# Weight rows loaded and split at other places of the program, and a third of one subtraction moved from GpSimd to VectorE, in a pre-LN block with dilated local attention and a squared-ReLU MLP

## The chip, the cores and the metric

The kernel runs on one core of a Trainium2 chip. The metric is device time in microseconds (us) of one execution; the median of three runs counts. Before the change it is 510.53 us (510.51 to 511.3). TensorE is called PE here, VectorE DVE, ScalarE ACT, GpSimd POOL, and SyncE, which issues nearly every DMA, SP, as in the profile.

## The reference

```
x = A_x                                              # 1 x 2048 x 512, f32
h = x + attn(layernorm(x), wqkv, wo)                 # 32 heads of 16
    # query s attends to keys s, s-2, ..., s-14; logits scaled by 16 ** -0.5,
    # those before the start are masked, softmax over the 8
h2 = h + mlp(layernorm(h), w1, b1, w2, b2)           # 512 -> 1792 -> 512
    # mlp: r = max(x @ w1 + b1, 0); (r * r) @ w2 + b2
```

## The kernel before

**Arithmetic.** Each matrix product is made of three PE products on numbers cut in two: `hi` copies a tile to the format fp32r on ACT (the high part, names ending in `_h`), `lo` subtracts that copy from the tile (the low part, `_l`), and PE adds high x high, low x high and high x low. "Splitting" a row of weights means a DMA of it to a buffer `raw`, one `hi` on ACT and one `lo` on POOL.

**Stages.** Tokens come in 16 tiles of 128.
1. The opening, 16 slots: layernorm, transposes and the q, k, v products of tiles 0 to 3, two head groups at a time.
2. Six passes of `first_phase` (`t0` = 4, 6, ... 14): the q, k, v products of two tiles each, in 12 slots numbered `m`.
3. The MLP of token blocks `u` = 0, 1, 2 (four tiles each): a slot `p` has the first product of weight column f = p (`mlp1`), the second product of f = p - 3 (`mlp2`), and at some p the attention's output product of a tile of the next block (`wo_product`).
4. The last block, `u` = 3, in another form of products.

Attention runs beside all this up to the middle of block 2: 64 units, each three DVE instructions of some 1.2 us (L339, L350, L373) and three additions on POOL (L407). q, k and v go to a DRAM buffer (`qkv_d`, from the tile `y2`, which has two buffers) and come back as windows `k`, `v`, `q`.

**What sets the order.** The order of every engine is written out by the program. A chore is put down for a slot: `at` (run at the start of the slot's end, list `due`), `midway`, `after` (run last, list `late`). `end_slot` runs `due`, then `pump`, which hands out attention until the planned DVE time reaches the planned PE time, then `late`. A chore on DVE that calls `dve(t)` therefore pushes attention back by t in the program. All DMAs but three stand in SP's one queue in the order of the program, and one whose source is not yet written holds up those behind it. Small tiles (rows of x, h, raw weights, parts) take turns in 15 buffers with the tag `row`.

**Lines of the change.** `weight_job` (L570) loads and splits one row of `wo` (4 jobs, 128x512) or of `w1` (16 jobs, 128x448); `first_phase` calls it at L1020. `split_w2` (L1069) splits row p of `w2` in slot p of block 0: `hi` to `big_h`, `lo` to a place in `big_l`, from where `stash` (L1078) stores it to DRAM one slot later for the later blocks. The place is taken again four rows later.

Of the kernel before, what the change touches and what calls it, by code (L numbers as in the profile page):

```python
# [52 lines left out]
HOLD = 1.0  # L53
XS = 6
WARM = 18


@with_exitstack
def block_kernel(ctx, tc, x, wqkv, wo, w1, b1, w2, b2, out):
    nc = tc.nc  # L60
# [39 lines left out]
    w2_h, w2_l = {}, {}  # L100

    def row(name, shape=(P, D), dt=F32):
        return work.tile(list(shape), dt, name=name, tag="row", bufs=ROWS)
# [9 lines left out]
    def at(delta, fn, *a):  # L113
        due.setdefault(now["slot"] + delta, []).append((fn, a))

    def after(delta, fn, *a):
        late.setdefault(now["slot"] + delta, []).append((fn, a))
# [4 lines left out]
    def end_slot(pe):  # L122
        now["pe"] += pe
        run(due)
        pump()
        run(amid)
        run(late)
        now["slot"] += 1
# [7 lines left out]
    def dve(t):  # L136
        now["dve"] += t
# [13 lines left out]
    def hi(dst, src):  # L151
        nc.scalar.copy(dst, src)  # L152
# [298 lines left out]
    def x_center(t):  # L451

        st = small.tile([P, 6], F32, name="st")
        mv = means[t] = small.tile([P, 2], F32, name="mv0", bufs=R)
        rs = rstd[t] = small.tile([P, 2], F32, name="rs0", bufs=R)
        nc.vector.bn_stats(st, xt[t])
        nc.vector.bn_aggr(mv, st)
        nc.vector.tensor_scalar(out=xt[t], in0=xt[t], scalar1=mv[:, 0:1], scalar2=None,
                                op0=ALU.subtract)
        dve(1.4)  # L460

    def x_rstd(t):
        mv, rs = means[t], rstd[t]
        nc.gpsimd.tensor_scalar(out=rs[:, 1:2], in0=mv[:, 1:2], scalar1=EPS, scalar2=None,
                                op0=ALU.add)
        nc.gpsimd.tensor_tensor(out=rs[:, 0:1], in0=rs[:, 1:2], in1=mhalf, op=ALU.pow)

    def x_T(t):
        tr = transposes(xt.pop(t))
        xT[t] = row("xh", (P, KB, P), F32R), row("xl", (P, KB, P), F32R)  # L470
        at(0, hi_T, tr, [xT[t][0]])
        after(0, lo_T, tr, [xT[t][0]], [xT[t][1]])
# [57 lines left out]
    def qkv_of(t, c, mid):  # L530

        ps = turn["mm"].tile("mm")
        xh, xl = xT[t]
        cs = slice(c * D, (c + 1) * D)
        mm3(ps, lambda k: xh[:, k, :], lambda k: xl[:, k, :],
            lambda k: wq_h[:, k, cs], lambda k: wq_l[:, k, cs], mid, 3 * KB // 2,
            lows_last=True)
        at(1, evac, t, 0, c, ps)

    def qkv(t, gp, mid=None):  # L540

        ps = turn["mm"].tile("mm")
        xh, xl = xT[t]
        mm3(ps[:, :3 * GP], lambda k: xh[:, k, :], lambda k: xl[:, k, :],
            lambda k: pair(wq_h, k, gp), lambda k: pair(wq_l, k, gp), mid, lows_last=t > 0)
        at(1, evac, t, gp, None, ps)
# [3 lines left out]
    def load_wqkv(gp, ks=range(KB), eng=nc.sync):  # L550
        for k in ks:
            if k % 2 == 0:
                tag = "pr" if (gp, k) in ((1, 2), (2, 0), (2, 2)) else "o"
                raws[gp] = att.tile([P, 2, D], F32, name="wraw", tag=tag, bufs=3)
            r = raws[gp, k] = raws[gp][:, k % 2, :3 * GP].rearrange("p (c n) -> p c n", c=3)
            src = wqkv[k * P:(k + 1) * P].rearrange("p (c n) -> p c n", c=3)
            eng.dma_start(r, src[:, :, gp * GP:(gp + 1) * GP])
# [9 lines left out]
    jobs = [(wo_h, wo_l, wo, k, 0, D) for k in range(KB)]  # L567
    jobs += [(w1_h, w1_l, w1, k, c * 448, 448) for k in range(KB) for c in range(4)]

    def weight_job():  # L570
        h, l, src, k, c0, cn = jobs.pop(0)
        raw = row("raw")
        nc.sync.dma_start(raw[:, :cn], src[k * P:(k + 1) * P, c0:c0 + cn])

        def split():
            hi(h[:, k, c0:c0 + cn], raw[:, :cn])
            after(0, lo, nc.gpsimd, l[:, k, c0:c0 + cn], raw[:, :cn], h[:, k, c0:c0 + cn])
        at(5, split)


    hs, hn = {}, {}
# [10 lines left out]
    def o_T(t):  # L592
        s, j = divmod(t, RI)
        pump(until=s)
        tr = transposes(o_t[s][:, j, :])
        if t % R == RI:

            ohl = att.tile([P, 2, KB, P], F32R, name="ohl", tag="o", bufs=3)
            oT[t] = ohl[:, 0], ohl[:, 1]
        else:  # L600
            oT[t] = row("oh", (P, KB, P), F32R), row("ol", (P, KB, P), F32R)
        at(0, hi_T, tr, [oT[t][0]])
        at(0, lo_T, tr, [oT[t][0]], [oT[t][1]])
# [79 lines left out]
    def wo_product(t, slots):  # L683
        ps = turn["mm"].tile("wo")
        oh, ol = oT.pop(t)
        mm3(ps, lambda k: oh[:, k, :], lambda k: ol[:, k, :],
            lambda k: wo_h[:, k, :], lambda k: wo_l[:, k, :], lows_last=t in OV)
        for n, (fn, a) in zip(slots, ((h_add, (t, ps)), (h_norm, (t,)), (add_b2, (t,)),
                                      (spill, (t,)))):
            (after if fn in (h_norm, spill) else at)(n + (fn is add_b2), fn, *a)  # L690
# [254 lines left out]
    warm = turn["tr"].tile("tr").rearrange("p (k c) -> p k c", k=KB)  # L945
    for n in range(WARM):
        nc.tensor.transpose(warm[:, n % KB, :], ident, ident)

    def start_T(t):
        x_T(t)  # L950
        run(due)
        run(late)

    def consts():
        nc.sync.dma_start(b1_sb, b1.rearrange("(f p) -> p f", p=P))
        nc.sync.dma_start(b2_sb, bass.AP(tensor=b2.tensor, offset=b2.offset, ap=[[0, P], [1, D]]))
# [20 lines left out]
    for n in range(16):  # L977
        gp, t = divmod(n, 4)
        qkv(t, gp, (lambda: start_T(t + 1)) if n < 3 else None)
        if n == 0:  # L980
            x_rstd(2)
            x_center(3)
        if n == 1:
            x_rstd(3)
        if n < 6:
            for k in (0, 1):
                at(0, hi_wqkv, n // 2 + 1, n % 2 * 2 + k)
                after(0, lo_wqkv, n // 2 + 1, n % 2 * 2 + k,
                      nc.gpsimd if k or n < 2 else nc.vector)
        if n == 1:  # L990
            load_wqkv(3)
        if n == 13:
            consts()
        if n in (5, 6, 12, 14):
            at(0, load_x, n - 1 if n < 7 else n // 2)
        if n in (8, 9):
            at(0, x_stats, n - 4)
        if n in (11, 12):
            at(0, x_norm, n - 7)
        if n in (13, 14):  # L1000
            x_T(n - 9)
        end_slot(2.09)
# [4 lines left out]
    def first_phase(t0):  # L1007
        def chores(m):
            if t0 + 3 < 16:
                if m in (0, 2):  # L1010
                    at(0, x_stats, t0 + 2 + m // 2)

                early = t0 == 12
                if m + early in ((4, 6) if t0 == R else (6, 7)):
                    at(0, x_norm, t0 + 2 + (m + early) // 7 if t0 > R else t0 + m // 2)
                if m in XT[early]:
                    x_T(t0 + 2 + XT[early].index(m))
            if t0 + 5 < 16 and m in (6, 9):
                at(0, load_x, t0 + 2 + m // 3)
            if jobs and m % 3 == 0:  # L1020
                at(0, weight_job)
            k = t0 // 2 * 12 - 72 + m
            if k == 19:
                dve(HOLD)
            for t in range(R):
                if k == OT[t]:
                    at(0, load_h, t)
                    o_T(t)
                if t in HV and k == HK[t][0]:
                    at(0, h_split, t)  # L1030
                    after(0, turn_dma, ("h", t))
                if t in HV and k == HK[t][1]:
                    at(0, turn_join, ("h", t))
                if k == WO[t]:
                    wo_product(t, (1, 3, 4, 6))
                    now["pe"] += 2.73
                if k == HT[t]:
                    (at(0, h_parts, t) if t in HV else h_T(t))
            if k in W2:
                at(0, load_w2, W2.index(k))  # L1040

        def half(m):
            end_slot(1.37)
            chores(m)

        for n in range(6):
            chores(2 * n)
            qkv_of(t0 + n % 2, n // 2, lambda: half(2 * n + 1))
            end_slot(1.37)
# [19 lines left out]
    def split_w2(f):  # L1069
        raw = raws.pop(f)  # L1070
        hi(w2_h[f], raw)
        if f < 12:
            place[f] = free.pop(0)
            w2_l[f] = big_l[:, place[f]]
            at(1, stash, f)
        after(0, lo, nc.gpsimd, w2_l[f], raw, w2_h[f])

    def stash(f):  # L1078
        nc.sync.dma_start(w2l_d[f], w2_l[f].bitcast(F32))
# [7 lines left out]
    for u in range(R - 1):  # L1087
# [45 lines left out]
        for p in range(FB + LAG):  # L1133
# [17 lines left out]
            if q >= 0:  # L1151
                f = fs[q]
# [93 lines left out]
```

## Time and profile before

| | us |
|---|---|
| median of the runs | 510.53 |
| the profiled execution | 510.24 |
| its span (first to last instruction) | 508.5 |
| PE busy | 498.6 (98%) |
| DVE busy | 375.2 (74%) |
| POOL busy | 361.4 (71%) |
| ACT busy | 305.3 (60%) |
| DMA queue of SP, share of 16 DMA engines | 68% |
| granted PE clock | 1.00 throughout |

PE counts as busy while one of several overlapping matmuls is in flight, so small stalls show less as idle time than as fewer matmuls in a stretch. The times of rows below are counted from the start of the span. A row of the timeline reads: start, duration of the group, engine, line, operation, output<-inputs, shape, count, and in brackets the idle time of that engine ahead of it with what ended it.

The stages lie at these places: the opening to 40 us, the six passes to 161 us, block 0 from 161 to 255 us, block 1 to about 340 us, block 2 to about 427 us.

### The profile page before, as it was taken

What the parts mean: (1) busy time and instruction counts of PE and PEld (TensorE: products, weight loads), DVE (VectorE), ACT (ScalarE), POOL (GpSimd) and SP (SyncE); (2) the same over time, 40 slices, a digit from 0 to 9 for tenths busy, and PEclk for the clock granted to TensorE, in tenths of its full rate; (3) what the DMA queues carried; (4) which work ended last, traced back from release to release, by engine and by line L of the source; (5) the groups of instructions that cost most, each with busy time, mean ns of one, the idle gap of its engine ahead of it and who ended that gap; (6) DMA issues with size and microseconds to landing.
All of it is one profiled execution on the core that took longest, in us unless ns stands there. A gap on an engine that the chain in (4) does not pass through costs nothing.

```text
span 508.5 us, 7542 instructions
## 1 busy us (share of the span) xinstructions
PE 498.6 (98%) x2422; PEld 420.5 (83%) x2422; DVE 375.2 (74%) x507; ACT 305.3 (60%) x558; POOL 361.4 (71%) x439
## 2 busy tenths in 40 slices
PE   8999999999999999999899999999999999999997
PEld 7998778888888887787688888888888888998986
DVE  6479899999999778986898989988951137732233
ACT  4635687577447747478454548756457847566541
POOL 5714789895776999989959777977896364685610
PEclk9999999999999999999999999999999999999999
DMA  8678889899698799789576756997572272444212
GB/s 271 189 212 204 245 290 302 245 307 303 201 228 253 253 273 278 215 216 291 166 248 207 216 147 165 257 252 244 161 173 63 80 212 83 169 123 144 64 43 83
DMA packets 109359, 102.61 MB, mean 202 GB/s; under 512 B 29448, under 2 KB 77832, under 8 KB 109320
## 3 DMA queue, kind: packets, MB, share of 16 engines
q1 hardware_dynamic: 108376, 101.61, 68.0%
q10 hardware_dynamic: 944, 0.52, 0.3%
q8 instruction: 19, 0.31, 0.2%
q14 instruction: 20, 0.16, 0.1%
HBM read 72.65 MB, written 24.25 MB: 191 GB/s over the span
## 4 chain that ended last, share of the span: by engine, by line
PE 66%; POOL 14%; DVE 2%; issue 2%; DMA 2%; ACT 1%; SPq 0%; POOLq 0%; ACTq 0%; DVEq 0%
PE mm L228 30%; PE acc L895 22%; PE wo L228 6%; PE mm L818 6%; POOL pr L407 5%; POOL rl L155 3%; POOL big_l L155 3%; PE tr L201 2%; POOL h L674 1%; DVE pr L350 1%; DMA q<-qkv_d 1%; DMA k<-qkv_d 1%; POOL o L407 1%; POOL w_x L155 1%; POOL rs L171 0%
## 5 line engine op out<-in xcount | busy, mean ns | idle before, releaser
L407 POOL TENSOR_TENSOR pr<-pr 128x512 f32<-128x512 f32 (+1 forms) x128 | 132.3, 1034 | 38.2 <-DVE pr L350 32.7
L228 PE MATMUL mm<-big_l,w_h 128*128 128x512 f32 x336 | 88.9, 391 | 0.7 <-ACT r L871 0.7
L350 DVE TENSOR_TENSOR pr<-ex,v 128x1024 f32<-128x1024 f32 x64 | 78.1, 1221 | 13.5 <-POOL o L407 10.1
L339 DVE TENSOR_TENSOR pr<-qp,k 128x1024 f32<-128x1024 f32 x64 | 76.8, 1200 | 9.3 <-ACT qp L268 8.4
L373 DVE TENSOR_REDUCE ex<-pr 128x64 f32<-128x1024 f32 x64 | 78.5, 1227 | 2.0
L228 PEld LDWEIGHTS mm<-big_l,w_h 128*128 128x128 f32 x336 | 62.8, 188 | 15.0 <-ACT r L871 2.0
L155 POOL TENSOR_TENSOR rl<-r,rh 128x512 fp32r<-128x512 f32 x42 | 55.6, 1326 | 14.9 <-ACT rh L152 14.9
L228 PE MATMUL mm<-big_l,xh 128*128 128x512 f32 (+1 forms) x208 | 55.8, 378 | 0.0
L228 PE MATMUL mm<-big_h,xh 128*128 128x512 f32 (+1 forms) x208 | 53.8, 379 | 1.3 <-ACT xh L152 1.3
L228 PE MATMUL mm<-big_h,xl 128*128 128x512 f32 (+1 forms) x208 | 52.7, 375 | 0.1
L895 PE MATMUL acc<-big_l,rh 128*128 128x512 f32 x190 | 52.2, 390 | 0.0
L895 PE MATMUL acc<-big_h,rh 128*128 128x512 f32 x190 | 52.1, 391 | 0.0
L895 PE MATMUL acc<-big_h,rl 128*128 128x512 f32 x190 | 51.7, 389 | 0.0
L871 ACT ACTIVATE r<-mm,b_sb 128x512 f32<-128x512 f32 x42 | 28.8, 685 | 33.6 <-PE mm L228 30.3
L228 PE MATMUL mm<-big_l,w_l 128*128 128x512 f32 x168 | 44.9, 389 | 0.0
L228 PEld LDWEIGHTS mm<-big_h,xh 128*128 128x128 f32 x208 | 37.6, 188 | 8.6 <-ACT xh L152 3.0
L228 PEld LDWEIGHTS mm<-big_h,xl 128*128 128x128 f32 x208 | 38.2, 188 | 6.4 <-DVE xl L155 0.5
L895 PEld LDWEIGHTS acc<-big_h,rl 128*128 128x128 f32 x190 | 35.7, 188 | 7.4
L895 PEld LDWEIGHTS acc<-big_l,rh 128*128 128x128 f32 x190 | 35.5, 188 | 7.4
L228 PEld LDWEIGHTS mm<-big_l,xh 128*128 128x128 f32 x208 | 37.5, 188 | 4.9
L895 PEld LDWEIGHTS acc<-big_h,rh 128*128 128x128 f32 x190 | 34.9, 188 | 6.7
L228 PEld LDWEIGHTS mm<-big_l,w_l 128*128 128x128 f32 x168 | 31.5, 188 | 6.6
(165 smaller groups left out, 917.8 us busy)
## 6 DMA issues: line engine op xcount, KB each, us to landing
k<-qkv_d SPq DMA_DIRECT2D x48, 288.0 KB, 3.1
v<-qkv_d SPq DMA_DIRECT2D x48, 288.0 KB, 3.6
qkv_d<-y SPq DMA_DIRECT2D x18, 512.0 KB, 5.1
big_l<-w2l_d SPq DMA_DIRECT2D x24, 256.0 KB, 3.1
xt<-in_A_x_dram SPq DMA_DIRECT2D x16, 256.0 KB, 4.7
q<-qkv_d SPq DMA_DIRECT2D x32, 128.0 KB, 3.7
h<-in_A_x_dram SPq DMA_DIRECT2D x16, 256.0 KB, 3.3
h_d<-h SPq DMA_DIRECT2D x16, 256.0 KB, 3.8
```

Source lines behind the costliest of these rows:

```text
L155: eng.tensor_tensor(out=dst, in0=src, in1=h, op=ALU.subtract)
L201: nc.tensor.transpose(tr[:, k, :], src[:, k * P:(k + 1) * P], ident)
L228: nc.tensor.matmul(ps, l(k), r(k), start=(n == 0), stop=(n == 3 * KB - 1))
L339: nc.vector.tensor_tensor(out=pr.rearrange("p i w h d -> p i w (h d)"), in0=qps["now"][:, j % 2].unsqueeze(2).to_broadcast([P, RI, W, GC]) ...
L350: nc.vector.tensor_tensor(out=p2, in1=vwin, op=ALU.mult, in0=e1[:, :, :, j * GH:(j + 1) * GH].unsqueeze(4).to_broadcast([P, RI, W, GH, DH]))
L373: nc.vector.tensor_reduce(out=lf[:, :, :, j * GH:(j + 1) * GH], in_=pr, axis=X, op=ALU.add)
L407: nc.gpsimd.tensor_tensor(out=dst, in0=p2[:, :, :w], in1=p2[:, :, w:2 * w], op=ALU.add)
L674: nc.gpsimd.tensor_tensor(out=h, in0=h, in1=b2_sb, op=ALU.add)
L818: nc.tensor.matmul(ps, sta[y][:, k], mov[x][:, k], start=(first and q == 0), stop=(last and q == len(terms) - 1), skip_group_check=True)
L871: nc.scalar.activation(r, ps, AF.Relu, bias=b1_sb[:, f:f + 1])
L895: nc.tensor.matmul(acc[j], l[:, j * P:(j + 1) * P], w[f], start=(first and n < len(js)), stop=(last and n >= len(terms) - len(js)))
```

## The change

Three edits.
- Three of the twenty weight jobs (rows 0 to 2 of `wo`) are put into the opening, at slots 4, 6 and 8, to be split four slots later. A pass has three jobs (m = 0, 4, 8) instead of four (m = 0, 3, 6, 9); the last two fall into the pass t0 = 14, which had none.
- The split of a job is run in `late`, behind the slot's attention, instead of in `due`, ahead of it.
- In block 0 the `lo` of rows f = 1, 4, 7, 10, 13 of `w2` goes to DVE instead of POOL, and 0.8 us of planned DVE time is booked for each.

```diff
+JOBS = 4, 6, 8
+JM = 0, 4, 8
...
-    def weight_job():
+    def weight_job(delay=5):
         h, l, src, k, c0, cn = jobs.pop(0)
...
-        at(5, split)
+        after(delay, split)
...
+        if n in JOBS:
+            at(0, weight_job, 4)
...
-            if jobs and m % 3 == 0:
+            if jobs and m in (JM if t0 < 14 else (0, 3, 5)):
                 at(0, weight_job)
...
-        after(0, lo, nc.gpsimd, w2_l[f], raw, w2_h[f])
+        eng = nc.vector if f % 3 == 1 else nc.gpsimd
+        after(0, lo, eng, w2_l[f], raw, w2_h[f])
+        if eng is nc.vector:
+            dve(0.8)
```

Line numbers of the changed kernel are higher by 2 in the helpers.

SP's queue in the opening, before. `qkv_d<-y` stores q, k and v of a pair of tiles, `qkv_d<-qkv_d` copies the rows ahead of the first token, `xt` is a tile of x, `k`, `q`, `v` are windows of attention.

```order
L487 DMA qkv_d<-qkv_d 2x8x64 x2
L497 DMA qkv_d<-y_90 128x3x128 x2
L247 DMA k<-qkv_d 128x704
L260 DMA q<-qkv_d 128x2x128
L247 DMA k<-qkv_d 128x704
L247 DMA v<-qkv_d 128x704 x2
L438 DMA xt<-in_A_x_dram 128x512 x2
L497 DMA qkv_d<-y_90 128x3x128 x2
L260 DMA q<-qkv_d 128x2x128
L487 DMA qkv_d<-qkv_d 2x8x64 x2
L497 DMA qkv_d<-y_90 128x3x128 x4
```

The same stretch of SP's queue with the change, from the store behind the first copy on:

```order
L575 DMA raw<-in_A_wo_dram 128x512
L499 DMA qkv_d<-y_90 128x3x128 x2
L249 DMA k<-qkv_d 128x704
L262 DMA q<-qkv_d 128x2x128
L249 DMA k<-qkv_d 128x704
L249 DMA v<-qkv_d 128x704 x2
L440 DMA xt<-in_A_x_dram 128x512 x2
L575 DMA raw<-in_A_wo_dram 128x512
L499 DMA qkv_d<-y_90 128x3x128 x2
L262 DMA q<-qkv_d 128x2x128
L489 DMA qkv_d<-qkv_d 2x8x64 x2
L575 DMA raw<-in_A_wo_dram 128x512
```

Each of the three loads stands right ahead of a store of `y`.

POOL at the start of block 0, before. `big_l<-raw,big_h` is the `lo` of a row of `w2` (the raw buffer's number tells the rows apart: 1871 is f = 0, 1980 f = 1, 2007 f = 2), `rl<-r,rh` the `lo` of a hidden column, `pr` and `o` the additions of an attention unit.

```order
L155 TENSOR_TENSOR big_l<-raw_1871,big_h 128x512
L155 TENSOR_TENSOR rl<-r,rh 128x512
L407 TENSOR_TENSOR pr<-pr 128x2x256
L407 TENSOR_TENSOR pr<-pr 128x2x128
L407 TENSOR_TENSOR o<-pr 128x2x64
L155 TENSOR_TENSOR big_l<-raw_1980,big_h 128x512
L155 TENSOR_TENSOR rl<-r,rh 128x512
```

POOL at the same place with the change (1869 is f = 0, 2007 f = 2):

```order
L157 TENSOR_TENSOR big_l<-raw_1869,big_h 128x512
L157 TENSOR_TENSOR rl<-r,rh 128x512 x2
L409 TENSOR_TENSOR pr<-pr 128x2x256
L409 TENSOR_TENSOR pr<-pr 128x2x128
L409 TENSOR_TENSOR o<-pr 128x2x64
L157 TENSOR_TENSOR big_l<-raw_2007,big_h 128x512
```

The subtraction of f = 1 has left POOL, and the next attention unit's additions stand behind the second hidden column's.

DVE in the middle of block 0, around the first `wo_product`, before. `ol` is the low part of the attention output of tile 4, `h<-wo,h` adds that product to the residual.

```order
L350 TENSOR_TENSOR pr<-ex,v 128x1024
L373 TENSOR_REDUCE ex<-pr 128x16x4
L339 TENSOR_TENSOR pr<-qp,k 128x1024
L350 TENSOR_TENSOR pr<-ex,v 128x1024
L373 TENSOR_REDUCE ex<-pr 128x16x4
L155 TENSOR_TENSOR ol<-pl,oh 128x512
L339 TENSOR_TENSOR pr<-qp,k 128x1024
L661 TENSOR_TENSOR h<-wo,h 128x512
```

DVE at the same place with the change (raw 2242 is f = 7):

```order
L352 TENSOR_TENSOR pr<-ex,v 128x1024
L157 TENSOR_TENSOR big_l<-raw_2242,big_h 128x512
L375 TENSOR_REDUCE ex<-pr 128x16x4
L341 TENSOR_TENSOR pr<-qp,k 128x1024
L157 TENSOR_TENSOR ol<-pl,oh 128x512
L352 TENSOR_TENSOR pr<-ex,v 128x1024
L375 TENSOR_REDUCE ex<-pr 128x16x4
L663 TENSOR_TENSOR h<-wo,h 128x512
```

The subtraction of f = 7 has come in, and two attention instructions that stood ahead of `ol` now stand behind it. From block 0 to the start of block 2 attention is about one unit later in the program than it was.

## The prediction

> **What bounds the kernel now.** I read the chain of waits by engine first, then windows, then each engine's timeline where PE's rate drops.
>
> ```profile
> PE 66%; POOL 14%; DVE 2%; issue 2%; DMA 2%; ACT 1%; SPq 0%; POOLq 0%; ACTq 0%; DVEq 0%
> ```
>
> Two thirds of the end hang on PE, and POOL is the only other engine that counts. To see where PE is held up I count weight loads (one a matmul), as busy time hides small stalls.
>
> ```profile
> core 0: us, PE busy (x) PEld busy (x) DVE busy (x) ACT busy (x) POOL busy (x), PEclk, DMA share, GB/s
> 175.22:196.98 21.76, 21.76 (x98) 18.02 (x96) 18.86 (x22) 12.45 (x21) 20.73 (x22) 1.00 0.80 254
> 196.98:254.82 57.84, 54.62 (x238) 43.04 (x236) 49.09 (x63) 37.15 (x61) 53.72 (x60) 1.00 0.84 230
> 253.00:339.00 86.00, 86.00 (x381) 71.00 (x382) 77.74 (x93) 53.18 (x91) 66.36 (x77) 1.00 0.75 212
> ```
>
> The first row is dense: 96 matmuls in 21.76 us, 0.227 each. The second has 236, of which 8 are short transposes: 228 x 0.227 = 51.7, with about 1.0 for the transposes 52.7. It lasts 57.84. So 5.1 us are lost in the second half of block 0, with POOL busy 93% of the time. Block 1 (third row) is dense again. What PE waited for:
>
> ```profile
> 205.66 1.21 PE L228 MATMUL wo<-wo_h,ol 128*128 128x512 f32 x4 [0.84 <-DVE ol L155]
> 235.53 1.21 PE L228 MATMUL mm<-big_l,w_h 128*128 128x512 f32 x4 [0.68 <-ACT r L871]
> 252.94 0.66 PE L201 MATMUL tr<-ident,hn 128*128 128x128 f32 x4 [1.45 <-ACT hn L196]
> ```
>
> And what held up those three engines:
>
> ```profile
> 202.53 1.23 DVE L350 TENSOR_TENSOR pr<-ex,v 128x1024 f32<-128x1024 f32 x1 [1.11 <-POOL o L407]
> 226.65 0.82 ACT L196 ACTIVATE hn<-h,rs 128x512 f32<-128x512 f32 x1 [3.11 <-POOL big_l L155]
> 234.79 0.69 ACT L871 ACTIVATE r<-mm,b_sb 128x512 f32<-128x512 f32 x1 [1.68 <-POOL rl L155]
> 252.08 0.81 ACT L196 ACTIVATE hn<-h,rs 128x512 f32<-128x512 f32 x1 [4.34 <-POOL rs L172]
> ```
>
> Each time it is POOL being behind. The other place where PE waits is the change from the first pass to the second, shown below.
>
> **The change, part by part.** *The lows of w2.* A low on POOL against the same kind of instruction on DVE (both inputs in SBUF, 128x512):
>
> ```profile
> L155 POOL TENSOR_TENSOR big_l<-raw,big_h 128x512 fp32r<-128x512 f32 x12 | 15.6, 1298 | 0.0
> L155 DVE TENSOR_TENSOR ol<-pl,oh 128x512 fp32r<-128x512 f32 x3 | 2.7, 894 | 0.0
> ...
> L407 POOL TENSOR_TENSOR pr<-pr 128x512 f32<-128x512 f32 x16 | 21.3, 1329 | 5.7 <-DVE pr L350 5.6
> L407 POOL TENSOR_TENSOR pr<-pr 128x256 f32<-128x256 f32 x17 | 13.0, 765 | 1.3
> L407 POOL TENSOR_TENSOR o<-pr 128x128 f32<-128x128 f32 x17 | 8.3, 489 | 1.3
> ...
> L339 DVE TENSOR_TENSOR pr<-qp,k 128x1024 f32<-128x1024 f32 x17 | 20.4, 1202 | 3.7 <-ACT qp L268 3.7
> L373 DVE TENSOR_REDUCE ex<-pr 128x64 f32<-128x1024 f32 x16 | 19.6, 1228 | 0.5
> L350 DVE TENSOR_TENSOR pr<-ex,v 128x1024 f32<-128x1024 f32 x16 | 19.5, 1220 | 5.2 <-POOL o L407 4.6
> ```
>
> These rows group block 0; the second number behind the bar is the mean in ns. Five lows take 5 x 1.30 = 6.5 us from POOL and add 5 x 0.89 = 4.5 to DVE. The 4.0 booked for them push one attention unit out of block 0, which takes its three additions (L407, 2.6 us) from POOL and 3.7 of work (L339, L350, L373) from DVE. So DVE has 0.8 more to do, POOL 9.1 less over 90 us, and the backlog that cost PE 5.1 us should not build up. The additions that now stand behind the second hidden column's low start later, but DVE takes their buffer again only three `pr` tiles on.
>
> The store of a low stands in SP's queue ahead of the next q:
>
> ```profile
> 177.76 0.32 SPq L1079 DMA_DIRECT2D w2l_d<-big_l  x1
> 179.11 0.42 SPq L260 DMA_DIRECT2D q<-qkv_d  x1
> 183.22 0.38 ACT L268 COPY qp<-q 128x256 f32<-128x256 f32 x1 [5.59 <-DMA q<-qkv_d]
> ```
>
> The store of f = 2 left at 177.76, once POOL had made that low; with f = 1 off POOL it can leave about 2 us earlier, q and ACT's copy with it. Behind a low on DVE stand attention and, for f = 7 and 13, `ol` or `h<-wo,h`. A DVE low waits for ACT's `hi`; DVE and ACT are nearly level there, and I put 0.6 us of what PE loses down as not recovered, between 0 (all recovered) and 5.1 (none, another engine being as late). I take a value near the low end since all four waits above end at POOL. Gain: 5.1 - 0.6 = 4.5.
>
> The unit of attention that is put off goes through block 1, where DVE has 77.74 of 86.00 busy with no loss at PE, to block 2; its cover is this:
>
> ```profile
> 380.00:400.00 20.00, 20.00 (x90) 16.57 (x89) 2.66 (x4) 14.04 (x25) 10.13 (x16) 1.00 0.23 61
> ```
>
> DVE is almost empty from 380 us, so it costs nothing; without that room it would cost its 3.7.
>
> A row speaks against the price of 0.89:
>
> ```profile
> 204.93 0.68 DVE L155 TENSOR_TENSOR ol<-pl,oh 128x512 fp32r<-128x512 f32 x1
> 212.15 1.09 DVE L155 TENSOR_TENSOR ol<-pl,oh 128x512 fp32r<-128x512 f32 x1
> 204.96 2.63 POOL L407 TENSOR_TENSOR pr<-pr 128x512 f32<-128x512 f32 x2
> 210.58 2.12 POOL L407 TENSOR_TENSOR pr<-pr 128x512 f32<-128x512 f32 x2
> ```
>
> The pair of additions that starts with the DVE low takes 2.63 instead of 2.12, and the DVE low that starts inside an addition takes 1.09 instead of 0.68: one delays the other by 0.4 to 0.5. Five lows so return up to 2.5 us to POOL or 2.0 to DVE; 9.1 - 2.5 = 6.6 is still more than the 5.1 lost. The Trainium skill (SBUF — State Buffer, Who interferes with whom) says why: a DVE instruction with two SBUF inputs and a GpSimd one that reads SBUF exclude each other for the whole instruction. By that rule a low could cost DVE up to a whole addition, 1.30 us, on top of its 0.68; the trace shows a third of that, and the full price is the first rival.
>
> *The opening.* Three loads of 256 KB go ahead of stores whose landing SP, and through the two buffers of `y2` ACT, waits for:
>
> ```profile
> 25.12 1.70 SPq L497 DMA_DIRECT2D qkv_d<-y  x2
> 32.29 1.23 SPq L487 DMA_DIRECT2D qkv_d<-qkv_d  x2
> 32.95 1.05 ACT L521 ACTIVATE y<-mm,rs 128x384 f32<-128x384 f32 x2 [5.96 <-DMA qkv_d<-y]
> 34.46 0.85 PE L228 MATMUL mm<-big_h,xh 128*128 128x384 f32 x4
> 22.00:26.00 4.00, 4.00 (x25) 4.00 (x24) 0.36 (x1) 1.54 (x3) 0.64 (x1) 1.00 0.78 229
> 26.00:30.00 4.00, 4.00 (x25) 4.00 (x24) 2.10 (x2) 0.58 (x1) 0.00 (x0) 1.00 0.99 289
> 30.00:34.00 4.00, 4.00 (x25) 4.00 (x24) 2.91 (x6) 1.05 (x3) 1.11 (x4) 1.00 0.45 138
> ```
>
> The stores of 25.12 land at 32.3. ACT has to empty slot 8's bank before PE needs it for slot 12, at 34.46: it ends 0.9 us ahead. The DMA engines are full from 26 to 30 us, where a load of 256 KB takes 0.9 us at 289 GB/s. The splits themselves (three `hi`, three lows on POOL) lie in idle time: ACT has 5.96 there, POOL 0.64 and 0.00 of 4 us busy. PE may lose something at 34.46, but it has time to give where the second pass begins:
>
> ```profile
> 56.30 0.59 ACT L523 COPY y<-mm 128x512 f32<-128x512 f32 x1 [0.93 <-DMA qkv_d<-y]
> 57.80 0.29 DVE L362 TENSOR_REDUCE sm<-ex 128x16 f32<-128x128 f32 x1 [2.19 <-ACT ex L396]
> 60.12 0.62 ACT L152 CAST wo_h<-raw 128x512 fp32r<-128x512 f32 x1 [2.35 <-DMA raw<-in_A_wo_dram]
> 61.76 1.20 PE L228 MATMUL mm<-big_h,xh 128*128 128x512 f32 x4 [0.60 <-ACT xh L152]
> 64.00 1.20 PE L228 MATMUL mm<-big_h,xl 128*128 128x512 f32 x4
> ```
>
> ACT's wait for a raw row at 60.12, ahead of `xh`, goes with the new order. But PE then waits for `xl`, which DVE makes at the end of a run that starts at 57.80 behind ACT's exp, itself behind a store that ACT waited for at 56.30. If the stores stay late from 33 to 56 us, the 64.00 moves by as much. Bounds: 0 (the loads fit into gaps and the exp comes no later) and 3.1 (three issues on SP of 0.42, as q's above, a transfer of 0.9 in the full stretch and half of that in each of the other two, all handed on). I take 1.5: the chain from store to load to store is serial, but two of the three loads fall where the engines are half idle.
>
> *Fewer jobs in a pass, at a slot's end.* From 64 us to 161 us PE has no stall, so less work on POOL and ACT there brings nothing, and the two jobs that the last pass gets cost ACT two `hi` ahead of block 0, and POOL two lows, where both have waits for others. These rows of `w1` are first used in slot 7 of block 0. Zero, at worst one `hi`, 0.62 as at 60.12.
>
> **The sum**, against the profiled execution, 510.24 (its span 508.5 and 1.74 around it): -4.5 + 1.5 = -3.0, that is 507.2. The median shown is 0.3 above that execution: **507.5**.
>
> **The rivals.**
> *DVE pays the full price.* Each low on DVE waits half an addition, 0.65, beside its 0.68, and holds POOL for 0.68. POOL's relief is 9.1 - 3.4 = 5.7, DVE gets 5 x 1.33 = 6.7 for the 3.7 that it loses, 3.0 more in a stretch where it has 8.7 idle, so `ol` and `h` stay late. About half of the 5.1 comes back: 510.5 - 2.6 + 1.5 = 509.4. For it: DVE busy 49.09 of 57.84; against it: `ol` stands one attention unit earlier in DVE's order.
> *The opening's chain decides, and the kernel is slower.* Each load ahead of a store whose landing SP waits for costs 0.4 of issue and 1.1 of transfer (229 GB/s): three make 4.5, all of it at 64.00. With the half gain of the first rival that is 510.5 + 4.5 - 2.6 = 512.4; it is slower than before from an opening loss above the gain in block 0. For it: the 5.96 and 0.93 on `qkv_d<-y`. Against it: 0.45 of the DMA engines' time used at 30 to 34 us.
> *It evens out:* block 0's waits pass to ACT's copies and DMA, 1.5 comes back, 1.5 is lost: 510.5.
> *The opening hides all:* 510.5 - 4.5 = 506.0, or less if the wait at 61 to 64 goes too.
>
> **How the numbers follow.** My forecast 52%, the opening hidden 14%, the full price 14%, evened out 9%, the slow opening 11%. A measurement of this kernel tells 0.2%, 1.0 us, from no change; so faster means below 509.5. The full price falls on that edge, mostly below: faster 0.78, within 0.2% 0.11, slower 0.11. The range reaches from most of the hidden opening to the full price and a little of the even case: 504.8 to 510.1.
>
> **What would show it.** Right: weight loads of block 0's second half at the dense rate, the waits on POOL `rs`, `rl` and `big_l` gone, the stash of f = 2 and the q behind it some 2 us earlier, ACT's `y` after 26.40 waiting longer than 5.96 on `qkv_d<-y`, and PE at the second pass's first `xl` 1 to 2 us later than 64.00. Wrong: DVE lows of over 1.2 us with POOL still full; stalls at `wo` that stay; or a PE gap at slot 12 of over 2 us.

## The result, and the profile after

The change makes the kernel slower: 513.77 us (median of four runs, 513.62 to 514.27) against 510.7 (510.51 to 511.3) for the kernel before on the same chip, a ratio of 1.0063 with a 95% interval of 1.0041 to 1.0085. The forecast was 507.5. The profiled execution's span is 512.0 us, 3.5 more than before's 508.5.

The view of windows counts PE's weight loads again, the stretches set to the same matmuls as before (first the dense stretch of block 0, then its second half, then block 1):

```profile
core 0: us, PE busy (x) PEld busy (x) DVE busy (x) ACT busy (x) POOL busy (x), PEclk, DMA share, GB/s
176.90:198.70 21.80, 21.80 (x98) 18.07 (x97) 19.17 (x23) 12.99 (x24) 21.05 (x22) 1.00 0.81 258
199.62:255.61 55.99, 54.09 (x239) 43.45 (x238) 48.24 (x62) 36.90 (x60) 48.19 (x54) 1.00 0.80 218
253.79:341.34 87.55, 86.47 (x381) 71.05 (x382) 77.49 (x92) 54.04 (x92) 66.80 (x79) 1.00 0.73 208
```

The second half of block 0 takes about 2 us less, with POOL busy for 48.19 us there instead of 53.72. Block 1, dense before in 86.00 us, now takes 87.55 for the same 382 weight loads. The stalls of PE in the timeline, from the opening to block 2, show where:

```profile
35.33 0.96 PE L230 MATMUL mm<-big_h,xh 128*128 128x384 f32 x4 [0.43 <-ACT y L523]
40.99 0.66 PE L203 MATMUL tr<-ident,xt 128*128 128x128 f32 x4 [1.22 <-ACT xt L198]
164.18 1.15 PE L230 MATMUL mm<-big_l,w_h 128*128 128x512 f32 x4 [0.92 <-DVE big_l L157]
233.26 1.21 PE L230 MATMUL wo<-wo_h,ohl 128*128 128x512 f32 x4 [0.54 <-ACT ohl L154]
237.14 1.20 PE L230 MATMUL mm<-big_l,w_h 128*128 128x512 f32 x4 [0.68 <-ACT r L873]
253.74 0.66 PE L203 MATMUL tr<-ident,hn 128*128 128x128 f32 x4 [0.69 <-ACT hn L198]
324.46 1.21 PE L230 MATMUL wo<-wo_h,ohl 128*128 128x512 f32 x4 [0.68 <-ACT ohl L154]
335.17 1.19 PE L230 MATMUL wo<-wo_h,ol 128*128 128x512 f32 x4 [0.40 <-DVE ol L157]
346.39 1.17 PE L230 MATMUL mm<-big_l,w_h 128*128 128x512 f32 x4 [0.92 <-DVE big_l L157]
```

Only those at 237 and 253 us were there before; the others are new, and the wait for `ol` near 206 is gone. The chain of waits by engine, which opened the prediction, says little this time: it breaks off early on its way back and holds work of a third of the span, nearly all of it PE's.

PE's instructions and their order are the same in all kernels here, so one matmul can be followed through the traces. The table gives by how much the start of the same matmul has moved against the trace of before, as increments from one place to the next: at 66.0 us of before (start of the second pass), 177.9 (block 0 under way), 254.8 (end of block 0), 345.9 (start of block 2). After that nothing moves by more than 0.02.

| | opening | to 178 | block 0 | block 1 | sum |
|---|---|---|---|---|---|
| the change | +1.49 | +1.45 | -2.15 | +2.72 | +3.51 |
| forecast | +1.5 | 0 | -4.5 | 0 | -3.0 |

Two places are as foreseen in sign, two that had been costed at nothing take 4.2 us.

**The new wait at 164 us.** Where the last pass ends, DVE makes four lows of `hn` that PE waits for. The next rows show ACT's `hi` of a weight row that the change put into this pass, then the four lows one by one, then what POOL ran beside them (`w_l` is the low of such a weight row).

```profile
154.20 0.55 ACT L154 CAST w_h<-raw 128x448 fp32r<-128x448 f32 x1
159.08 0.96 DVE L157 TENSOR_TENSOR big_l<-pl,big_l 128x256 fp32r<-128x256 f32 x1 [1.05 <-ACT big_l L154]
159.96 0.68 DVE L157 TENSOR_TENSOR big_l<-pl,big_l 128x256 fp32r<-128x256 f32 x1
160.56 1.51 DVE L157 TENSOR_TENSOR big_l<-pl,big_l 128x256 fp32r<-128x256 f32 x1
162.00 1.37 DVE L157 TENSOR_TENSOR big_l<-pl,big_l 128x256 fp32r<-128x256 f32 x1
159.02 0.74 POOL L409 TENSOR_TENSOR pr<-pr 128x256 f32<-128x256 f32 x1
159.84 0.52 POOL L409 TENSOR_TENSOR o<-pr 128x128 f32<-128x128 f32 x1
160.33 1.46 POOL L676 TENSOR_TENSOR h<-h,b_sb 128x512 f32<-128x512 f32 x1
161.75 1.34 POOL L157 TENSOR_TENSOR w_l<-raw,w_h 128x448 fp32r<-128x448 f32 x1
```

Each of the four lows ends 0.28 us after one of the four POOL instructions does, so while POOL runs one instruction behind the other, DVE gets through one low for each of them. Together the four take 4.29 us. In the kernel before, POOL ran nothing beside the fourth low, which took 0.41 us, the first met only the end of an addition and took 0.57, and the four took 2.95:

```profile
156.95 2.95 DVE L155 TENSOR_TENSOR big_l<-pl,big_l 128x256 fp32r<-128x256 f32 x4 [0.64 <-ACT big_l L152]
157.81 1.47 POOL L674 TENSOR_TENSOR h<-h,b_sb 128x512 f32<-128x512 f32 x1
```

The lows also start 2.13 us later than before, 0.64 more than the opening's shift of 1.49. That part is ACT's: its `hi` of 154.20 stands ahead of its copies of `hn`, and ACT is busy nearly without a gap from there on. In `opening_only`, an experiment below without weight rows in this pass, the lows start exactly as late as the opening's shift there. So PE's operand comes 0.64 + 1.34 us later than the opening alone would have it, of which PE loses 1.45.

The same meeting takes place at the end of block 1, where there are no weight rows. The first row is the kernel before, where POOL ran only the small `rs` instructions beside the four lows, and the second the change, where the additions of an attention unit that has come later run beside them. PE's wait at 346 us is for these lows.

```profile
337.88 1.42 DVE L155 TENSOR_TENSOR big_l<-pl,big_l 128x256 fp32r<-128x256 f32 x4
341.13 3.32 DVE L157 TENSOR_TENSOR big_l<-pl,big_l 128x256 fp32r<-128x256 f32 x4
```

**ACT's two long waits.** ACT's timeline has these rows, at the split of an `o` tile for the transposing DMA:

```profile
221.39 1.05 ACT L618 COPY pl<-o 128x1024 uint16<-128x1024 uint16 x1 [7.13 <-POOL o L409]
312.07 1.05 ACT L618 COPY pl<-o 128x1024 uint16<-128x1024 uint16 x1 [7.17 <-POOL o L409]
```

In the kernel before, the copy of 216.27 has no wait. `o_split` calls `pump(until=s)`, which hands out attention until the eight groups of that `o` are done. By the program's own count all eight are done there in the kernel before; with the 0.8 us bookings seven are, in block 0 and again in block 1, so the last unit is forced in directly ahead of the split, and ACT stands until POOL has added it up, with exp and the hidden columns behind it. In block 1 PE has lost nothing up to this wait. It loses 1.5 us around the stalls at 324 and 335 us that follow, and 1.2 at the lows just shown.

**The opening.** First the three loads on SP's queue, with the store behind the first of them and the window `k` that waits for this store to land, and ACT's wait for the second store; then windows:

```profile
19.50 0.39 SPq L575 DMA_DIRECT2D raw<-in_A_wo_dram  x1
19.99 0.91 SPq L499 DMA_DIRECT2D qkv_d<-y  x2
23.09 0.33 SPq L249 DMA_DIRECT2D k<-qkv_d  x1
26.35 0.67 SPq L575 DMA_DIRECT2D raw<-in_A_wo_dram  x1
35.37 0.35 SPq L575 DMA_DIRECT2D raw<-in_A_wo_dram  x1
34.70 1.05 ACT L523 ACTIVATE y<-mm,rs 128x384 f32<-128x384 f32 x2 [6.89 <-DMA qkv_d<-y]
```

```profile
30.00:34.00 4.00, 4.00 (x25) 4.00 (x24) 1.80 (x3) 0.00 (x0) 0.76 (x2) 1.00 0.97 294
34.00:38.00 4.00, 3.57 (x21) 3.25 (x20) 3.86 (x8) 2.11 (x5) 2.59 (x6) 1.00 0.44 105
38.00:42.00 4.00, 2.78 (x18) 2.46 (x17) 3.93 (x7) 2.35 (x4) 1.29 (x1) 1.00 1.02 301
```

The DMA engines are now full from 30 to 34 us as well (0.97, before 0.45). ACT waits 6.89 for the store in place of 5.96, and PE loses time from 34 us on. The same store and window before:

```profile
19.80 0.90 SPq L497 DMA_DIRECT2D qkv_d<-y  x2
21.85 0.34 SPq L247 DMA_DIRECT2D k<-qkv_d  x1
```

With a load ahead of the store, `k` leaves 3.10 us after it instead of 2.05. The next store takes no longer to land than before (6.93 us from 27.11 to 34.04, before 7.17), so the second load costs only the 0.76 us for which it holds SP's queue. The two come to about the 1.75 us by which SP goes on later (34.04 against 32.29).

### The profile page after: what moved, and what is told of

Its sections match the earlier page's. It is cut to its first block, busy times and chain, and to the rows that moved or that the text cites. A ratio compares the mean times of both kernels' runs of the same rounds, so it can differ in the third digit from the quotient of the medians.

```text
span 512.0 us, 7540 instructions
## 1 busy us (share of the span) xinstructions
PE 499.8 (98%) x2422; PEld 421.1 (82%) x2422; DVE 381.6 (75%) x512; ACT 304.6 (59%) x558; POOL 356.0 (70%) x434
## 6 DMA issues: line engine op xcount, KB each, us to landing
qkv_d<-y SPq DMA_DIRECT2D x18, 512.0 KB, 4.7
```

## The experiments

Fourteen kernels. Kernels sent together share the runs of the kernel before, whose median was 509.96 to 510.18 in these groups. Shifts are those of the table above, from each kernel's trace. The opening differs from one execution to the next: with the opening of before the shift in it was -0.99 to +0.42 us, with the change's +0.59 to +1.65, and with the loads behind the stores +0.17 and +1.47. So the opening is judged by the medians of the runs, the later places by the traces.

### The two halves of the change

`jobs_only` is the change without the edit of `split_w2`; `lows_only` is the kernel before with that edit alone.

```diff
-        eng = nc.vector if f % 3 == 1 else nc.gpsimd
-        after(0, lo, eng, w2_l[f], raw, w2_h[f])
-        if eng is nc.vector:
-            dve(0.8)
+        after(0, lo, nc.gpsimd, w2_l[f], raw, w2_h[f])
```

> Only the weight rows move (three in the opening, three in a pass, split at a slot's end); all lows of w2 stay on POOL, and nothing is booked for them. Theory A (three separate places): the second pass starts 1.5 us later, block 0 starts another 1.1 later, block 0 loses its 5.1 as before and block 1 nothing: 510.7 + 2.6 = 513.3. Theory B (block 0's waits on POOL are waits for work whose start doesn't depend on PE, so a PE that comes later waits less there): 510.7 to 511.5.

> Only the five lows on DVE, with 0.8 booked for each; the weight rows as before. Theory A: a gain of 2.0 in block 0 and a loss of 2.6 in block 1, as in the change: 511.3. Theory B (the lows do gain, and the weight rows cost it): 507.5. In both the 7 us of ACT at the split of o near 219 and near 310 are there, if they come from the booking.

| | median | ratio, 95% interval | opening | to 178 | block 0 | block 1 |
|---|---|---|---|---|---|---|
| jobs_only | 513.78 | 1.0073, 1.0052 to 1.0094 | +0.96 | +1.58 | +0.63 | +0.01 |
| lows_only | 509.84 | 0.9997, 0.9982 to 1.0011 | -0.84 | +0.01 | -2.69 | +2.87 |

All of the slowdown is in the weight rows; for the 0.63 us that they cost in block 0 (0.85 in `after_nobook` below) nothing here shows a cause. The other half by itself is worth nothing: block 0 gains 2.69 and block 1 gives 2.87 back. The 7 us waits of ACT are in `lows_only` (7.13 at 217.04 and 7.10 at 307.77), so they belong to it.

### Lows without the booking, and the booking without lows

`lows_nobook` and `after_nobook` are `lows_only` and the change with the two lines `if eng is nc.vector: dve(0.8)` taken out. `book_only` is the kernel before with the booking alone:

```diff
         after(0, lo, nc.gpsimd, w2_l[f], raw, w2_h[f])
+        if f % 3 == 1:
+            dve(0.8)
```

> The five lows on DVE, and nothing booked for them, so the order of attention is the one before. Theory A (the booked 4.0 us put one attention unit behind its due time; the split of o then waits 7 us on ACT with exp and the hidden columns behind it): both 7 us waits are gone, block 1 loses nothing and block 0 gains 3 to 4.5: 506 to 508. Rival P (each low on DVE takes 1.2 to 1.6 us and delays POOL as well, whatever is booked): block 0 gains 2.0 at most and block 1 loses much as in the change: 509 to 511.

> The whole change, without the 0.8 booked for each low on DVE. Theory A: 513.8 less 2.6 in block 1 and less 1 to 2 in block 0: 509 to 510.5. Rival P: 513 to 514.

> The kernel before, with 0.8 us booked on DVE's account for f = 1, 4, 7, 10, 13 and every low of w2 on POOL as before: only the place of attention in the order changes. Theory C (the gain in block 0 comes from the attention unit that the booking puts off, not from the lows; it is paid back in block 1 by the forced unit ahead of the split of o): PE comes 2 to 3 us sooner at 253 us and has lost that again at 343 us, time as before, 509.5 to 511. Rival (the lows make the gain, the booking only the loss): block 0 gains nothing and block 1 loses 2.7: 513.

| | median | ratio, 95% interval | opening | to 178 | block 0 | block 1 |
|---|---|---|---|---|---|---|
| lows_nobook | 510.88 | 1.0015, 1.0000 to 1.0030 | +0.33 | -0.03 | +0.08 | -0.07 |
| after_nobook | 514.08 | 1.0076, 1.0056 to 1.0097 | +1.65 | +1.19 | +0.85 | -0.07 |
| book_only | 510.23 | 1.0004, 0.9991 to 1.0016 | -0.11 | -0.03 | -2.25 | +1.94 |

My theory A fell here. Without the booking block 1 loses nothing, as it said, but block 0 gains nothing either. And the booking alone, with every low still on POOL, gains 2.25 in block 0 and loses 1.94 in block 1, with ACT's waits in its trace:

```profile
218.74 1.05 ACT L616 COPY pl<-o 128x1024 uint16<-128x1024 uint16 x1 [8.43 <-POOL o L407]
308.92 1.05 ACT L616 COPY pl<-o 128x1024 uint16<-128x1024 uint16 x1 [6.99 <-POOL o L407]
```

So most of what block 0 gains is the attention unit that was put off. The lows moved to DVE add 0.4 beside it (2.69 against 2.25), which is within the scatter (2.14 to 3.03 in the six traces with both), and nothing without it. The timeline of `lows_nobook`, DVE and then PE, and its window of the second half of block 0:

```profile
202.05 1.14 DVE L155 TENSOR_TENSOR big_l<-raw,big_h 128x512 fp32r<-128x512 f32 x1
205.93 0.73 DVE L155 TENSOR_TENSOR ol<-pl,oh 128x512 fp32r<-128x512 f32 x1
206.72 1.19 PE L228 MATMUL wo<-wo_h,ol 128*128 128x512 f32 x4 [1.20 <-DVE ol L155]
```

```profile
196.98:254.82 57.84, 54.19 (x238) 43.04 (x237) 51.01 (x66) 37.62 (x62) 51.41 (x58) 1.00 0.83 231
```

A low stands in DVE's queue ahead of `ol`, and PE waits 1.20 for `ol`, more than the 0.84 of before. POOL has gone from 53.72 to 51.41 busy, DVE from 49.09 to 51.01, and PE's weight loads from 236 to 237, which is nothing.

### POOL's relief without DVE's load

`relief` tells whether POOL's backlog was the cause at all. It leaves out four lows of `w2` but for 16 columns.

```diff
-        after(0, lo, nc.gpsimd, w2_l[f], raw, w2_h[f])
+        cut = slice(0, 16 if f in (1, 4, 7, 10) else D)
+        after(0, lo, nc.gpsimd, w2_l[f][:, cut], raw[:, cut], w2_h[f][:, cut])
```

> The kernel before, but for f = 1, 4, 7 and 10 POOL makes the low of 16 columns of 512 only, and DVE none: the lows of w2 are left out there and stale values stand in their place. This takes some 4 x 1.2 us from POOL and gives DVE nothing. Theory R (block 0's 5.1 us are POOL's backlog; the lows on DVE take it away and cost DVE as much): 506 to 507.5. Theory S (the waits on POOL end with POOL, but what sets them is the chain of attention through DVE, which a lighter POOL does not shorten): 509 to 510.

Measured: 507.63 us, ratio 0.9957 (0.9940 to 0.9973); block 0 -2.59, block 1 -0.11, all else within 0.15. The window of the same stretch and the wait that is left at its end:

```profile
196.98:254.82 57.84, 56.08 (x249) 45.33 (x248) 49.96 (x65) 36.86 (x60) 50.02 (x59) 1.00 0.80 224
```

```profile
250.45 0.66 PE L201 MATMUL tr<-ident,hn 128*128 128x128 f32 x4 [1.47 <-ACT hn L196]
```

POOL was the cause of at least half: 4 x 1.08 us (1.30 of a low less 0.22 of its 16 columns) off POOL bring 2.59 of the 5.1, and the wait that is left goes back to POOL too, as ACT's `hn` there waits 4.36 us for `rs`. Handing the same work to DVE takes that gain away.

### Can the unit be paid back earlier?

`lows_repay0` is `lows_only` with the 4.0 us taken off the account again at the start of block 1, so that the split of `o` finds all eight groups done; `lows_repay8` does so at slot 8, `book_repay0` at the start with all lows on POOL.

```diff
             if u < 2 and p == FB - 2:
                 dve(HOLD)
+            if u == 1 and p == 0:
+                dve(-4.0)
```

> Five lows on DVE with 0.8 booked for each, and the 4.0 taken off the account again at the start of block 1, so that the split of o at its slot 10 finds the attention done. Theory C: block 0's gain of 2.8 stays, block 1 loses nothing: 507.5. Rival (block 1's DVE, busy 77.74 of 86.00 us before the change, has no room for the unit wherever it stands): block 1 loses 2 to 3 as before, 510.

> As the last, with all lows on POOL as before. If the lows on DVE help beside the booking, this is 0.5 to 1.5 slower than the last; if they don't, the same or faster: 507.5.

> As lows_repay0, with the 4.0 taken off the account at slot 8 of block 1, two slots ahead of the split that needs the attention. If the stall at 297 us of lows_repay0 came from the unit standing ahead of a low of o, block 1 loses 1 or less and the time is 508 to 508.7; if block 1 has no room for the unit anywhere, 509.5 to 510.

| | median | ratio, 95% interval | opening | to 178 | block 0 | block 1 |
|---|---|---|---|---|---|---|
| lows_repay0 | 509.62 | 0.9996, 0.9982 to 1.0010 | -0.99 | -0.00 | -2.82 | +2.03 |
| book_repay0 | 510.10 | 0.9998, 0.9983 to 1.0014 | +0.15 | -0.03 | -2.45 | +1.53 |
| lows_repay8 | 513.64 | 1.0066, 1.0047 to 1.0085 | +0.42 | -0.03 | -2.76 | +5.04 |

The first two lose nothing at the split of block 1, but 1.5 to 2.0 near 296 us, where PE waits for `ol`; in `lows_repay0`:

```profile
295.54 1.20 PE L228 MATMUL wo<-wo_h,ol 128*128 128x512 f32 x4 [1.75 <-DVE ol L155]
```

This is another loss than the change's. Counted by DVE's L339 instructions between the same two matmuls (254.8 and 345.9 us of before), block 1 holds 17 units in the kernel before, in the change, in `lows_only` and in `book_only`, but 18 in the three kernels here. The change hands one unit into block 1 and one on to block 2; its loss comes with the same number of units, each later than before, in the forced unit and in the lows of `hn` that take 3.32 us (3.3 in `lows_only` and `book_only` too, 1.42 again in `lows_repay0`). One unit more had no room either, in the two places tried. `lows_repay8` puts it at a worse place, and its loss holds something else, shown in the last section.

### The last pass

`jobs_no_last` is the change with no weight row in the last pass; the first two passes take four each instead of three.

```diff
-            if jobs and m in (JM if t0 < 14 else (0, 3, 5)):
+            if jobs and m in ((0, 3, 6, 9) if t0 < 8 else JM):
```

> The whole change, but the 17 weight rows that are left after the opening go into the passes 4 to 12 (4, 4, 3, 3, 3), none in the last one. Theory D (the last pass's two lows on POOL hold up the four lows of hn on DVE, 4.29 us for 2.95, and PE waits for them at 164 us): PE's shift against before at 161 to 165 us stays at 1.5 to 1.7 in place of 2.6, time 512 to 512.7. Rival (the shift there is only the opening's lateness, met again by a wait that does not depend on it): no change, 513.8.

Measured: 511.97 us, 1.0041 (1.0025 to 1.0058), against 1.0063 for the change; the increment to 178 us is -0.02, and the four lows of `hn` are back:

```profile
157.53 3.01 DVE L157 TENSOR_TENSOR big_l<-pl,big_l 128x256 fp32r<-128x256 f32 x4 [0.58 <-ACT big_l L154]
```

The two rows in the last pass cost 1.1 us by the ratios and 1.2 to 1.6 by the traces (the increments to 178 us of the change, `jobs_only` and `after_nobook`). By the rows above, 0.96 us of the lows' delay is POOL's low of a weight row, 0.64 is ACT's `hi`, and some 0.4 is the first low, which now met a whole addition; these were not tried apart.

### The opening

`opening_only` has the opening rows alone: `jobs_no_last` with all lows on POOL and nothing booked. `opening_behind` issues the loads at the slot's end, behind the store and attention's loads; `opening_pool` issues them on POOL's queue.

```diff
         if n in JOBS:
-            at(0, weight_job, 4)
+            after(0, weight_job, 4)
```

> Only the three weight rows in the opening (loads ahead of the stores of slots 4, 6 and 8, split at a slot's end); the other 17 in passes 4 to 12, none in the last; all lows of w2 on POOL, nothing booked. The rest of the loss that the lows and the last pass's rows do not explain: 1.5 to 2.0 slower than before, 511.5 to 512. If the opening costs nothing by itself and the losses of the change's parts only add up by chance: 510.

> As opening_only, with the three loads issued at a slot's end, behind the store and the attention's loads on SP's queue. Theory E (the store, whose landing ACT and SP wait for, stands behind the load's issue): two thirds or more come back, 510 to 510.6. Theory F (the load's 256 KB take the DMA engines' time in a full stretch, wherever they are issued): 511.5 to 512.

> As opening_only, with the three loads issued on POOL's queue, where POOL is idle. Theory E: SP's queue is that of before, 510 to 510.6. Theory F: 511.5 to 512, as opening_only.

| | median | ratio, 95% interval |
|---|---|---|
| opening_only | 512.01 | 1.0035, 1.0022 to 1.0049 |
| opening_behind | 510.38 | 1.0001, 0.9988 to 1.0014 |
| opening_pool | 511.64 | 1.0023, 1.0012 to 1.0033 |

Here one theory was half right. Issued behind the store, the loads cost nothing that can be told; so the order matters and not the bytes, against theory F. But SP's issue time is not the whole price: on POOL's queue, where the loads leave at 18.95 and 22.64, still ahead of the stores they hurt, two thirds of the cost stay by the medians, though the intervals overlap. The traces show the landing of the first store directly: `k` leaves 2.06 us after it in `opening_behind`, 2.48 to 3.10 in the five traces with the change's opening, and 3.78 in `opening_pool`. `opening_only`'s window and then `opening_pool`'s show the DMA engines full in both at 30 to 34 us:

```profile
30.00:34.00 4.00, 4.00 (x25) 4.00 (x24) 1.69 (x3) 0.00 (x0) 0.64 (x2) 1.00 0.95 303
```

```profile
30.00:34.00 4.00, 4.00 (x25) 4.00 (x24) 1.51 (x4) 0.00 (x0) 0.06 (x1) 1.00 0.96 309
```

By these rows what counts is which transfer reaches the engines first, though the DMA engines' own order was not looked at. The Trainium skill (Trainium Kernel Development and Optimization, Key Constraints) states that DMAs of the different queues run on the same 16 engines, and that another queue saves issue time only. The run agrees, 1.0023 against 1.0035. The three loads were not tried one by one. `opening_behind`'s profiled execution was the longest of its twelve runs (511.52), so its trace is not used for the size.

### The change with both losses taken out

`mended` is `jobs_no_last` with `opening_behind`'s edit: lows on DVE and the booking as in the change.

> The whole change with both of its losses taken out: the opening's three loads issued at a slot's end behind the store, and none of the other rows in the last pass; lows on DVE and the booking as in the change. If the parts add up, the sum of opening_behind (1.0001) and lows_only (0.9997) is 1.000: 510. If the parts interact, 508.5 or 511.5.

Measured: 510.06 us, 0.9998 (0.9987 to 1.0010); block 0 -2.14, block 1 +2.76. The parts add up, and what is left of the change is worth nothing. The split at a slot's end, the second edit, is in `opening_behind` and here too, so it costs nothing that can be told. None of the kernels that compute the whole reference beats the one before.

## Why the prediction was wrong

**The opening: +1.5, right in mechanism, and in size partly by luck.** The trace of the change has +1.49, other traces with the same opening +0.59 to +1.65, and `opening_only` +1.8 by its ratio (0.35% of 510). The mechanism was the one named, loads ahead of stores that are waited for, but the price was put on the wrong load. Two of the three did leave where the engines were half idle (0.38 of their time used from 18 to 22 us, 0.44 from 34 to 38), and one of these, the first, cost its store 1.05 us on the way to landing. The one in the full stretch cost its store's landing nothing.

**Two rows into the last pass: costed at zero, 0.62 at worst; 1.45 measured in the change.** I looked at what stood on ACT's and POOL's own queues and at when the rows are first used. The 0.62 of one `hi` came (0.64). What failed beyond it is that a low on POOL also slows a low on DVE beside it. I had a price (0.4 to 0.5 a meeting) two paragraphs earlier, but applied it to the five lows of `w2` alone. Here the lows met are those that PE waits for next, and the price was higher: 1.42 us for four of them alone, 2.95 where three of them and 4.29 where all four ended only behind a POOL instruction. The weight row's low alone made the fourth take 1.37 instead of 0.41. The Trainium skill (SBUF — State Buffer, Who interferes with whom) has such a pair exclude each other for the whole instruction. At this place the rows agree, and my third was too little.

**The put-off unit: costed at zero; 1.9 to 2.9 in block 1.** It did go through block 1 to block 2, as foreseen: block 1 holds 17 units as before, and block 2 one more. The step that failed is "it costs nothing". Each `o` has a due time, the split that `pump(until=s)` guards, and a unit that comes later is forced in there; and its additions on POOL then stand beside the lows of `hn`, which cost 1.2 us of it. DVE's 77.74 of 86.00 us without a loss at PE was read as room, and the due time was not looked for.

**Block 0: a gain of 4.5; 2.15 measured in the change.** The step that failed is the account "DVE 0.8 more, POOL 9.1 less". Its 9.1 was 6.5 of lows and 2.6 of the unit's additions. The lows were worth 0.08 us the wrong way by themselves (`lows_nobook`), the unit 2.25 (`book_only`). That all four waits end at POOL was true, and `relief` shows that POOL's load is the cause of at least half; but DVE was next in line, and a low placed ahead of `ol` in its queue gives back what POOL saves. The means of the lows that DVE took, in the change:

```profile
L157 DVE TENSOR_TENSOR big_l<-raw,big_h 128x512 fp32r<-128x512 f32 x4 | 4.6, 1150 | 1.0 <-ACT big_h L154 1.0
L157 DVE TENSOR_TENSOR w_x<-raw,w_x 128x512 fp32r<-128x512 f32 x1 | 0.7, 682 | 0.0
```

That is 5.3 us for 4.5 forecast, so the price of a low was a small part of the error. That its place was the larger part is argued from the wait for `ol` in `lows_nobook`; no run moved the lows to other places of DVE's queue.

**The rivals.** The slower one had the sign and the place of the opening, but a price of 4.5 for what cost 1.5 to 1.8. The one of the full price had DVE as the engine that turns late, and saw half of block 0's gain go; it did not see block 1.

**The signs to look for.** Some of those for a right forecast were seen: ACT's `y` waited longer (6.89), PE at the second pass's first `xl` came 1.5 late (65.51), and PE's wait at the end of block 0, which had come from POOL's `rs`, shrank from 1.45 to 0.69. Others were not: block 0's second half did not reach the dense rate (230 x 0.227 and 1.0 for the transposes make 53.2 us, it took 55.99), PE's wait for `r` stayed at 0.68, and there was still a stall at `wo`, which had been named as a sign of being wrong. None of the signs lay in block 1 or at the end of the last pass, the two places that had been costed at nothing.

## What to carry to other kernels

Where an account of planned time puts work off, find the next point that forces it before you call it free: the cost moves to that due time, and a stretch without stalls is not a stretch with room. Work that moves in time also meets other work: look at which subtractions on DVE will then have POOL beside them. Before work is moved off a late engine, ask what stands behind it in the queue of the engine that takes it; leaving the work out altogether in one run tells what the relief can be worth. A load into a stretch that waits for a store's landing belongs behind that store, and in this kernel another queue was no way round it.

## What the runs showed of the hardware

In `lows_repay8` PE stands for one wait of 3.25 us, and then it runs at half rate. Windows, then PE's rows:

```profile
298.00:300.00 2.00, 1.51 (x4) 1.23 (x5) 1.57 (x2) 0.38 (x1) 1.92 (x3) 0.56 0.39 138
300.00:302.00 2.00, 2.00 (x7) 1.58 (x6) 1.40 (x2) 0.00 (x0) 0.79 (x1) 0.59 0.44 149
302.00:304.00 2.00, 2.00 (x11) 1.63 (x10) 1.93 (x3) 0.00 (x0) 1.42 (x2) 1.00 0.27 55
```

```profile
298.49 2.08 PE L228 MATMUL wo<-wo_h,ol 128*128 128x512 f32 x4 [3.25 <-DVE ol L155]
300.36 1.68 PE L228 MATMUL mm<-big_l,w_h 128*128 128x512 f32 x4
301.87 1.09 PE L228 MATMUL mm<-big_l,w_l 128*128 128x512 f32 x4
```

The granted clock is 0.56 and 0.59 in the two stretches after the wait. Eight matmuls take the 3.38 us from 298.49 to 301.87 instead of 8 x 0.227, which costs 1.6 us beyond the stall itself. None of the shorter stalls in the other kernels' blocks, up to 1.76 us, did this. The Trainium skill (TensorE: Matmul & The Clock Gate, What's actually happening) has the clock halved after an idle window of about 3.4 us and given back after as much busy time. The 3.38 us agree with the second; the wait, 3.25 by the profile, is close to the first but does not measure it, as no wait here lies between 1.76 and 3.25 us. So this stall cost half as much again as it lasted.
